# Third x chunk transposed between the slab products, and W4's 64-row rests in pairs of chunks

## The chip, the cores and the metric

The kernel runs on one NeuronCore of a Trainium2 chip. The metric is the device time of one execution in microseconds, the median over the runs shown. TensorE (PE) multiplies, VectorE (DVE) and ScalarE (ACT) work on the results, GpSimd (POOL) does small side work, and SyncE (SP) issues most DMAs.

## The reference

One input x of 2048 rows and 640 columns goes through two branches, and a gate mixes them. Types are bfloat16.

```python
x = A_x                                          # (1, 2048, 640)
g = sigmoid((x * gate_w).sum(-1, keepdims=True))
# branch A: linear attention, 32 heads of 20
q, k, v = split(x @ wqkv)
pq, pk = phi(q), phi(k)                          # phi(t) = (t + 1 if t > 0 else exp(t)) + 1e-6
kv  = einsum("bhsd,bhse->bhde", pk, v); z = pk summed over s
a = (einsum("bhqd,bhde->bhqe", pq, kv) / (einsum("bhqd,bhd->bhq", pq, z) + 1e-6)) @ wo
# branch B: mixer block and MLP
h  = gelu(layernorm(x) @ w1)                     # 640 -> 640
hs = four column groups of h, shifted by +1, -1, +2, -2 rows, @ w2
x1 = x + hs
b  = x1 + gelu(layernorm(x1) @ w3) @ w4          # 640 -> 1728 -> 640
out = g * a + (1 - g) * b
```

## The kernel before, in words

The 2048 rows are 16 chunks of 128. The 640 columns are five slabs of 128 (`DC = 5`). The hidden 1728 columns of the MLP are 13 full slabs (`NF = 13`) and a rest of 64 (`FT = 64`). The order is written out by hand: each engine runs its instructions in the order in which the program records them. Four PSUM buffers (`PP[0]` to `PP[3]`, 1024 float32 columns each) go round in turn by `alloc` and `release`.

**The start.** K = x @ wk needs x with its columns on the partitions (`xT`). The first three chunks are loaded as they are and transposed on PE (`x_tr`, L322 to L328): five transposes into two PSUM buffers, a copy of three of them by DVE (L327) and of two by ACT (L328). All other chunks come by transposing DMAs on SP's queue (`load_xT` in `late_loads`, shown in the profile as L159), between plain loads of x (`load_x`, L156). A one-column memset of `xT` at chunk 3's place (L333) stands ahead of `late_loads`, and the first transposing DMA writes over it, so that DMA waits for DVE to reach the memset. `k_mm(c, p, dc)` (L258, products on L260) multiplies chunk c with slab dc of the K weights `wkg`, in 512 and 130 columns (two of them for the gate and the row sum). The weights' slabs 0 to 2 come on ACT's queue (L166), 3 and 4 on SP's (L173). After the five slabs of a chunk, `k_post` makes phi with ACT (L252) and DVE (L255, L256). A PSUM buffer comes free when DVE is done with it. `g_unit` products (L269, for x-transposed times phi(K)) stand between the chunks.

**The middle.** `kv_unit` (L441) forms the per-head products in six groups of up to 120 columns, the last group having 40; `m_unit` (L455) multiplies each group with its rows of wo. Before the change the sixth group is 120 wide as well: its weights are columns 520 to 639 of wv, and `kvT` of it is padded with zeros to 120 columns. `den_unit` (L468) makes the denominators in tiles of 32 columns of the array, and `rexp_unit` spreads their reciprocals in tiles of 32 rows. `w1_unit` (L420, products on L426) is the first MLP-like product of branch B, `w2_unit` (L557) the second.

**The end.** For each half (t = 0 and 2, eight chunks each) `w3_pair` (L572, products L576) makes twelve slabs of the hidden layer for 512 rows, `w3_rest` (L581, products L585) the thirteenth. `w3_tail` (L590, products L595) makes the rest of 64 columns, for both halves at once, as pairs of 64-column tiles of the array that run side by side. `a_unit(c)` (L602, products L606) is branch A's product for one chunk, scaled by ACT (L609) and added to x1 by DVE (L611). `w4_group` (L620) takes four chunks: 26 products of full height each (`main`, L632: 13 slabs in 512 and 128 columns) and one rest of 64 rows (`rest`, L638), also as pairs of tiles. The rests of all four chunks stand together, at the end of the sums of the first two and the start of those of the last two. `fin` (L615) adds on DVE and sends the output. In the last group the final chunk is split into its 512 and its 128 columns, the second part opened by a product with zero-padded weights `w4z` (L667).

Of the kernel before, what the change touches and what calls it, by code (L numbers as in the profile page):

```python
# [16 lines left out]
def kernel(  # L17
# [14 lines left out]
    P = 128  # L32
# [3 lines left out]
    NCH = S // P  # L36
    DC = D // P
    GW = 120
    NG = 6
    G5 = D - GW  # L40
    gof = [g * GW for g in range(5)] + [G5]
    gw_ = [GW] * 5 + [D - 5 * GW]
    NF = F // P
    FT = F - NF * P
    EPS = 1e-5
# [27 lines left out]
    x_sb = RXH[:, 0:NCH * D].rearrange("p (c d) -> p c d", c=NCH)  # L73
    hsT = RXH[:, NCH * D:NCH * D + DC * (S + 4)].rearrange("p (j s) -> p j s", j=DC)
    h2T = RXH[:, 0:2 * NF * 512].rearrange("p (t f s) -> p t f s", t=2, f=NF)
    KP = 648
    wkg = RA[:, 0:DC * KP].rearrange("p (j d) -> p j d", j=DC)
    o_ = DC * KP
# [20 lines left out]
    o_ += 3 * D  # L99
    gas = [RXH[:, o_ + 2 * i * D:o_ + 2 * (i + 1) * D].bitcast(F32) for i in range(2)]  # L100
    shs = sb("shs", 1024)
    h2x = [RXH[:, 2 * NF * 512:2 * NF * 512 + 512], shs[:, 0:512]]
    w4z = shs[:, 512:640]
    w1x = sb("w1x", DC * P)[:].rearrange("p (j d) -> p j d", j=DC)
    kvT = sb("kvT", 6 * GW)[:].rearrange("p (g d) -> p g d", g=6)
    warm = sb("warm", 512)
# [85 lines left out]
    for f in range(4):  # L192
# [2 lines left out]
                                pattern=[[1, P]], channel_multiplier=-4)  # L195
        nc.gpsimd.affine_select(out=e4, in_=e4, compare_op=ALU.is_ge, fill=0.0, base=3,
                                pattern=[[-1, P]], channel_multiplier=4)
    nc.gpsimd.memset(kvT[0:GW, 5, gw_[5]:GW], 0.0)
    nc.gpsimd.memset(hsT[:, :, 0:4], 0.0)
    nc.gpsimd.memset(hsT[:, :, S:S + 4], 0.0)  # L200

# [83 lines left out]
    def late_loads():  # L285
        load_xT(3, 4)
        load_xT(4, 5)
        load_x(3, 4)
        load_xT(5, 6)
        load_xT(6, 7)  # L290
        load_x(4, 6)
        load_xT(7, 8)
        load_xT(8, 10)
        load_x(6, 9)
        load_xT(10, 11)
        load_xT(11, 13)
        load_x(9, 12)
        load_xT(13, 16)
        load_x(12, 16)
        rows = lambda w, a, b: w[:, a:b].rearrange("(j p) d -> p j d", p=P)  # L300
        sp.dma_start(wq, rows(A_wqkv, 0, D))
        sp.dma_start(w1, rows(B_w1, 0, D))
        sp.dma_start(wv, rows(A_wqkv, 2 * D, 3 * D))
        sp.dma_start(wo6[0:GW, 0:5, :], A_wo[0:5 * GW, :].rearrange("(g r) d -> r g d", r=GW))
        sp.dma_start(wo6[0:GW, 5, :], A_wo[G5:D, :])
        sp.dma_start(w2[:, 0:4, :], B_w2.rearrange("(g c) d -> c g d", c=CG)[0:P])
        for g in range(4):
            sp.dma_start(w2[32 * g:32 * (g + 1), 4, :], B_w2[CG * g + P:CG * (g + 1), :])
        w1g = w1.rearrange("p k (g c) -> p k g c", c=CG)
        w1x4 = w1x.rearrange("p k (g c) -> p k g c", g=4)  # L310
        for g in range(4):
            nc.gpsimd.tensor_copy(w1x4[:, :, g, :], w1g[:, :, g, P:CG])
# [9 lines left out]
    def x_tr(c, a, b):  # L322
        ta, tb = PP[a][:, 0:512].bitcast(BF16), PP[b][:, 0:512].bitcast(BF16)
        for dc in range(DC):
            t, k = (ta, dc) if dc < 3 else (tb, dc - 3)
            nc.tensor.transpose(t[:, k * P:(k + 1) * P], x_sb[:, c, dc * P:(dc + 1) * P], ident[:])  # L326
        nc.vector.tensor_copy(xT[:, 0:3, c * P:(c + 1) * P], ta[:, 0:3 * P].rearrange("p (j s) -> p j s", j=3))  # L327
        act(xT[:, 3:5, c * P:(c + 1) * P], tb[:, 0:2 * P].rearrange("p (j s) -> p j s", j=2), ACT.Copy)  # L328

    for _ in range(3):  # L330
        alloc()
    x_tr(0, 3, 2)
    nc.vector.memset(xT[:, 0, 3 * P:3 * P + 1], 0.0)  # L333
    late_loads()
    x_tr(1, 1, 2)
    k_mm(0, 0, 0)
    k_mm(1, 1, 0)
    k_mm(0, 0, 1)
    k_mm(1, 1, 1)
    x_tr(2, 3, 2)  # L340
    k_mm(2, 2, 0)
    k_mm(2, 2, 1)
    for c in range(3):
# [96 lines left out]

    def kv_unit():  # L441
        p = alloc()
        for g in range(NG):
            w = gw_[g]
            for dc in range(DC):
                mm(PP[p][0:GW, g * P:g * P + w], lhsT=wv[:, dc, gof[g]:gof[g] + GW], rhs=Gp[:, dc, g * GW:g * GW + w],  # L446
                   start=(dc == 0), stop=(dc == DC - 1))
        b0 = PP[p][0:GW, 0:512].rearrange("p (g d) -> p g d", d=P)[:, :, 0:GW]
        nc.vector.tensor_tensor(kvT[0:GW, 0:4, :], b0, bmask[0:GW, :].unsqueeze(1).to_broadcast([GW, 4, GW]),
                                op=ALU.mult)  # L450
        nc.vector.tensor_tensor(kvT[0:GW, 4, :], PP[p][0:GW, 512:512 + GW], bmask[0:GW, :], op=ALU.mult)
        nc.vector.tensor_tensor(kvT[0:GW, 5, 0:w], PP[p][0:GW, 640:640 + w], bmask[0:GW, GW - w:GW], op=ALU.mult)
        release(p)

    def m_unit(g):  # L455
        p = alloc()
        for (n0, n1) in COLS:
            mm(PP[p][0:GW, n0:n1], lhsT=kvT[0:GW, g, :], rhs=wo6[0:GW, g, n0:n1], start=True, stop=True)  # L458
        w = gw_[g]
        act(Mnat[0:w, g, :], PP[p][0:w, 0:D], ACT.Copy)  # L460
        release(p)

    def m_move():
        sp.dma_start(Mscr[0:5 * GW, :].rearrange("(g r) d -> r g d", r=GW), Mnat[0:GW, 0:5, :])
        sp.dma_start(Mscr[5 * GW:D, :], Mnat[0:gw_[5], 5, :])
        sp.dma_start(Mp, Mscr[:, :].rearrange("(q j) d -> q j d", j=DC))

    def den_unit():  # L468
# [60 lines left out]
    w4v = B_w4[0:NF * P, :].rearrange("(f p) d -> p f d", p=P)  # L529
    sp.dma_start(w4[0:FT, NF, :], B_w4[NF * P:F, :])  # L530
    sp.dma_start(w4[FT:2 * FT, NF, :], B_w4[NF * P:F, :])
    nc.gpsimd.memset(w4z[0:FT, :], 0.0)
    sp.dma_start(w4z[FT:2 * FT, :], B_w4[NF * P:F, 512:D])
    sp.dma_start(w4[:, 0:7, :], w4v[:, 0:7, :])
    sp.dma_start(w4[:, 7:NF, :], w4v[:, 7:NF, :])

# [44 lines left out]
    def w3_rest(t):  # L581
# [4 lines left out]
                   rhs=lnxT[:, dc, (t + k) * 512:(t + k + 1) * 512], start=(dc == 0), stop=(dc == DC - 1))  # L586
        act(h2T[:, :, NF - 1, :], PP[p][:].rearrange("p (k s) -> p k s", k=2), ACT.Gelu_apprx_tanh)
        release(p)

    def w3_tail():  # L590
        p = alloc()
        for u in range(2):
            for dc in range(DC):
                for k in range(2):
                    mm(PP[p][FT * k:FT * (k + 1), u * 512:(u + 1) * 512], lhsT=w3[:, dc, NF * P:F],  # L595
                       rhs=lnxT[:, dc, (2 * u + k) * 512:(2 * u + k + 1) * 512], start=(dc == 0), stop=(dc == DC - 1),
                       tile_position=(0, FT * k), skip_group_check=True)
        for u in range(2):
            act(h2x[u], PP[p][:, u * 512:(u + 1) * 512], ACT.Gelu_apprx_tanh)
        release(p)  # L600

    def a_unit(c):  # L602
# [14 lines left out]
                                       op0=ALU.mult, op1=ALU.add)  # L617
        (aq if n0 else sp).dma_start(out2[c * P:(c + 1) * P, n0:n1], oc[:, n0:n1])

    def w4_group(t, g, ahead, last):  # L620
        hx = h2x[t // 2]
        its = [(i, k) for i in (2 * g, 2 * g + 1) for k in range(2)]
        cs = [4 * t + 4 * k + i for (i, k) in its]
        ps = [None] * 4
        oc = [ocs[(ocn[0] + m) % 3] for m in range(4)]
        ocn[0] += 4

        def main(m, parts=COLS):
            i, k = its[m]
            for fc in range(NF):  # L630
                for (n0, n1) in parts:
                    mm(PP[ps[m]][:, n0:n1], lhsT=h2T[:, k, fc, i * P:(i + 1) * P], rhs=w4[:, fc, n0:n1],  # L632
                       start=(m < 2 and fc == 0), stop=(m >= 2 and fc == NF - 1))

        def rest(m, n0, n1):
            i, k = its[m]
            q = slice(FT * k, FT * (k + 1))
            mm(PP[ps[m]][:, n0:n1], lhsT=hx[q, i * P:(i + 1) * P], rhs=w4[q, NF, n0:n1], start=(m >= 2),  # L638
               stop=(m < 2), tile_position=(FT * k, 0))

        ps[0] = alloc()
        main(0)
        a_unit(cs[2])
        a_unit(cs[3])
        ps[1] = alloc()
        main(1)
        ps[2], ps[3] = alloc(), alloc()
        for (ms, (n0, n1)) in zip(((0, 1, 2, 3), (2, 1, 0) if last else (2, 3, 0, 1)), COLS):
            for m in ms:
                rest(m, n0, n1)  # L650
        for m in range(2):
            fin(cs[m], ps[m], 0, D, oc[m])
            release(ps[m])
        main(2)
        fin(cs[2], ps[2], 0, D, oc[2])
        release(ps[2])
        for c in ahead:
            a_unit(c)
        if not last:
            main(3)  # L660
            fin(cs[3], ps[3], 0, D, oc[3])
            release(ps[3])
            return
        main(3, COLS[:1])
        fin(cs[3], ps[3], 0, 512, oc[3])
        ps[3] = alloc()
        mm(PP[ps[3]][:, 512:D], lhsT=hx[:, its[3][0] * P:(its[3][0] + 1) * P], rhs=w4z, start=True, stop=False)  # L667
        main(3, COLS[1:])
        fin(cs[3], ps[3], 512, D, oc[3])

    sq = [(j, 1) for j in range(DC)]
    for t in (0, 2):
        for tt in (t, t + 1):
            for fc in range(0, NF - 1, 2):
                w3_pair(tt, fc)
                pop(ln2_d, 3)
                if sq and not ln2_d:
                    scale_q(*sq.pop(0))
        w3_rest(t)
        if t == 0:  # L680
            assert not ln2_d
            w3_tail()
        while ln2_d:
            pop(ln2_d)
        while sq:
            scale_q(*sq.pop(0))
        a_unit(4 * t)
        a_unit(4 * t + 4)
        w4_group(t, 0, (4 * t + 2, 4 * t + 6), False)
        w4_group(t, 1, (), t == 2)  # L690


# [28 lines left out]
```

## Time and profile before

| what | value |
|---|---|
| time, median of 5 runs | 265.0 us (264.74 to 265.33) |
| the profiled execution's own time | 265.33 us |
| its span, first to last instruction | 263.6 us |
| granted TensorE clock, mean | 1.000 |
| PE busy | 258.8 us, 98% of the span |
| DVE, ACT, POOL busy | 126.8, 109.7, 36.2 us |

The profile is of one execution. The span is what the engines' records cover; the execution's own time is 1.7 us longer. Matmuls overlap in the pipeline and their ends are modelled, so start-to-start times, or the pieces of the chain, tell what a product takes; single durations don't.

### The profile page before, as it was taken

The numbers are of one execution on the slowest core, as the hardware profiler recorded it, in microseconds if no ns is written. First come the engines' busy times: TensorE is split into PE (matmuls) and PEld (weight loads), VectorE is DVE, ScalarE is ACT, GpSimd is POOL, SyncE is SP. The second block draws the span as 40 slices with busy tenths as digits, with TensorE's granted clock in tenths as the row PEclk, the third lists the DMA queues.
The fourth block names the chain that finished last, engine by engine and source line by source line (L and its number), as shares of the span: only waits on it lengthen the run. The fifth ranks groups of instructions, "written<-read, shape, count | busy, mean of one in ns | idle before, by whom it ended". The sixth has DMA issues, their size and how long they took to land.

```text
span 263.6 us, 4185 instructions
## 1 busy us (share of the span) xinstructions
PE 258.8 (98%) x1666; PEld 136.1 (52%) x1666; DVE 126.8 (48%) x227; ACT 109.7 (42%) x163; POOL 36.2 (14%) x120
## 2 busy tenths in 40 slices
PE   7999999999999999999999999999999999999995
PEld 3555555555564445554444455555544445555552
DVE  2387759888995257999920023422310002334133
ACT  3466654555353771334977432102034445202200
POOL 7000043030200000436770000000000000000000
DMA  6799994552242059992552000200200000010011
GB/s 203 156 211 257 367 241 106 100 52 47 52 55 47 4 140 372 339 189 50 100 103 50 0 2 0 75 27 0 77 25 0 0 2 0 0 51 26 25 52 50
DMA packets 42372, 24.07 MB, mean 91 GB/s; under 512 B 31137, under 2 KB 41585, under 8 KB 42353
## 3 DMA queue, kind: packets, MB, share of 16 engines
q1 hardware_dynamic: 41767, 23.28, 36.6%
q10 hardware_dynamic: 586, 0.53, 0.6%
q8 instruction: 13, 0.21, 0.4%
q14 instruction: 6, 0.05, 0.0%
HBM read 12.98 MB, written 3.44 MB: 62 GB/s over the span
## 4 chain that ended last, share of the span: by engine, by line
PE 98%; ACT 0%; DVE 0%; issue 0%
PE pp L632 22%; PE pp L576 20%; PE pp L260 9%; PE pp L606 8%; PE pp L426 8%; PE pp L561 8%; PE pp L269 8%; PE pp L393 8%; PE pp L585 2%; PE pp L316 1%; PE pp L638 1%; PE pp L595 1%; PE pp L446 1%; PE pp L458 1%; PE pp L326 1%; PE pp L472 0%
## 5 line engine op out<-in xcount | busy, mean ns | idle before, releaser
L632 PE MATMUL pp<-RB,RXH 128*128 128x512 bf16 (+1 forms) x416 | 58.6, 299 | 0.0
L576 PE MATMUL pp<-lnxT,RA 128*128 128x512 bf16 x240 | 52.1, 379 | 0.0
L632 PEld LDWEIGHTS <-RXH 128*128 128x128 bf16 x416 | 31.8, 98 | 24.5
L576 PEld LDWEIGHTS <-RA 128*128 128x128 bf16 x240 | 23.4, 98 | 28.1
L578 ACT ACTIVATE RXH<-pp 128x1024 bf16<-128x1024 f32 x24 | 24.3, 1020 | 30.5 <-PE pp L576 30.5
L252 ACT ACTIVATE eb<-pp 128x640 bf16<-128x640 f32 (+1 forms) x26 | 21.4, 829 | 25.0 <-PE pp L393 16.1
L609 ACT ACTIVATE RXH<-pp,g_all 128x640 f32<-128x640 f32 x16 | 12.7, 795 | 45.4 <-PE pp L606 45.4
L611 DVE SCALAR_TENSOR_TENSOR RPK<-RPK,omg,RXH 128x640 f32<-128x640 f32 x8 | 7.1, 884 | 41.4 <-ACT RXH L609 41.4
L269 PE MATMUL pp<-RPK,RXH 128*128 128x512 bf16 (+1 forms) x160 | 25.2, 299 | 0.0
L260 PE MATMUL pp<-RA,RXT 128*128 128x512 bf16 (+1 forms) x160 | 24.2, 303 | 0.5 <-ACT RXT L328 0.5
L393 PE MATMUL pp<-RXT,RA 128*128 128x512 bf16 x100 | 23.2, 379 | 0.0
L606 PE MATMUL pp<-Mp,pqT 128*128 128x512 bf16 (+1 forms) x160 | 23.0, 299 | 0.0
L611 DVE SCALAR_TENSOR_TENSOR RXT<-RXT,omg,RXH 128x640 f32<-128x640 f32 x8 | 7.1, 884 | 32.0 <-ACT RXH L609 32.0
L561 PE MATMUL pp<-w,RXH 128*128 128x512 bf16 (+1 forms) x160 | 21.9, 299 | 0.0
L426 PE MATMUL pp<-lnxT,RB 128*128 128x512 bf16 x80 | 18.3, 379 | 0.0
L269 PEld LDWEIGHTS <-RXH 128*128 128x128 bf16 x160 | 12.7, 98 | 10.4
L260 PEld LDWEIGHTS <-RXT 128*128 128x128 bf16 x160 | 12.6, 99 | 10.2 <-DVE RXT L327 0.8
L606 PEld LDWEIGHTS <-pqT 128*128 128x128 bf16 x160 | 12.3, 98 | 9.8 <-issue 0.4
L561 PEld LDWEIGHTS <-RXH 128*128 128x128 bf16 x160 | 12.3, 98 | 9.6
L393 PEld LDWEIGHTS <-RA 128*128 128x128 bf16 x100 | 11.1, 117 | 9.1
L255 DVE TENSOR_SCALAR eb<-eb 128x640 bf16<-128x640 bf16 (+1 forms) x26 | 9.4, 363 | 11.5 <-ACT eb L252 11.5
L256 DVE SCALAR_TENSOR_TENSOR RPK<-pp,eb 128x640 bf16<-128x640 f32 x16 | 13.2, 824 | 2.1
(112 smaller groups left out, 238.4 us busy)
## 6 DMA issues: line engine op xcount, KB each, us to landing
out_dram<-RXH SPq DMA_DIRECT2D x15, 160.0 KB, 1.8
RA<-in_B_w_dram SPq DMA_DIRECT2D x5, 432.0 KB, 6.8
RA<-in_A_wqkv_dram SPq DMA_DIRECT2D x2, 800.0 KB, 6.8
RB<-in_B_w_dram SPq DMA_DIRECT2D x1, 1120.0 KB, 9.7
RXH<-in_A_x_dram SPq DMA_DIRECT2D x2, 480.0 KB, 4.8
RB<-in_B_w_dram SPq DMA_DIRECT2D x1, 960.0 KB, 11.2
RB<-in_B_w_dram SPq DMA_DIRECT2D x1, 800.0 KB, 8.5
Mp<-Mscr SPq DMA_DIRECT2D x1, 800.0 KB, 4.3
```

Source lines behind the costliest of these rows:

```text
L252: act(e[:, 0:n], src, ACT.Exp)
L256: nc.vector.scalar_tensor_tensor(dst, src, 0.0, e[:, 0:n], op0=ALU.max, op1=ALU.add)
L260: mm(PP[p][:, n0:n1], lhsT=xT[:, dc, c * P:(c + 1) * P], rhs=wkg[:, dc, n0:n1], start=(dc == 0), stop=(dc == DC - 1))
L269: mm(PP[p][:, n0:n1], lhsT=x_sb[:, c, i * P:(i + 1) * P], rhs=pk[:, c, n0:n1], start=(c == 0), stop=(c == NCH - 1))
L393: mm(PP[p][:, tt * 512:(tt + 1) * 512], lhsT=wqp[:, dc, j], rhs=xT[:, dc, t0:t0 + 512], start=(dc == 0), stop=(dc == DC - 1))
L426: mm(PP[p][:, tt * 512:(tt + 1) * 512], lhsT=lh, rhs=lnxT[:, dc, t0:t0 + 512], start=(dc == 0), stop=(dc == DC - 1))
L561: mm(PP[p][:, n0:n1], lhsT=hsT[:, fc, 2 + c * P:2 + (c + 1) * P], rhs=w2[:, fc, n0:n1], start=(fc == 0), stop=(fc == DC - 1))
L576: mm(PP[p][:, k * 512:(k + 1) * 512], lhsT=w3[:, dc, (fc + k) * P:(fc + k + 1) * P], rhs=lnxT[:, dc, t * 512:(t + 1) * 512], start=(dc == ...
L578: act(h2T[:, t % 2, fc:fc + 2, :], PP[p][:].rearrange("p (k s) -> p k s", k=2), ACT.Gelu_apprx_tanh)
L606: mm(PP[p][:, n0:n1], lhsT=pqT[:, j, c * P:(c + 1) * P], rhs=Mp[:, j, n0:n1], start=(j == 0), stop=(j == DC - 1))
L611: nc.vector.scalar_tensor_tensor(x1(c), x1(c), omg[:, c:c + 1], ga, op0=ALU.mult, op1=ALU.add)
L632: mm(PP[ps[m]][:, n0:n1], lhsT=h2T[:, k, fc, i * P:(i + 1) * P], rhs=w4[:, fc, n0:n1], start=(m < 2 and fc == 0), stop=(m >= 2 and fc == N ...
```

## The change

Four places differ.

- At the start, `x_tr(1)` is recorded ahead of the memset and `late_loads`, and `x_tr(2)` goes between the products with slab 0 and those with slab 1 of chunks 0 and 1. On DVE the memset is now behind the copy of the second chunk.
- `kv_unit` and `m_unit` treat the sixth group as 40 wide, without padding.
- `w3_tail` is gone; its products for one half stand at the end of `w3_rest`, once for each half.
- `w4_units` replaces `w4_group`. It takes two chunks: two `a_unit`s, then the four rest products (two chunks, two widths), which open the sums, then the full-height products. The last pair still splits its final chunk into 512 and 128 columns; its second part is opened by a rest product, and `w4z` with its memset and load is gone.

```diff
     x_tr(0, 3, 2)
+    x_tr(1, 1, 2)
     nc.vector.memset(xT[:, 0, 3 * P:3 * P + 1], 0.0)
     late_loads()
-    x_tr(1, 1, 2)
     k_mm(0, 0, 0)
     k_mm(1, 1, 0)
+    x_tr(2, 3, 2)
     k_mm(0, 0, 1)
     k_mm(1, 1, 1)
-    x_tr(2, 3, 2)
     k_mm(2, 2, 0)
     k_mm(2, 2, 1)
...
     def kv_unit():
         p = alloc()
-        for g in range(NG):
-            w = gw_[g]
+        for g in range(6):
+            w = gsz[g]
             for dc in range(DC):
-                mm(PP[p][0:GW, g * P:g * P + w], lhsT=wv[:, dc, gof[g]:gof[g] + GW], rhs=Gp[:, dc, g * GW:g * GW + w],
+                mm(PP[p][0:w, g * P:g * P + w], lhsT=wv[:, dc, g * GW:g * GW + w], rhs=Gp[:, dc, g * GW:g * GW + w],
                    start=(dc == 0), stop=(dc == DC - 1))
...
     def m_unit(g):
         p = alloc()
+        w = gsz[g]
         for (n0, n1) in COLS:
-            mm(PP[p][0:GW, n0:n1], lhsT=kvT[0:GW, g, :], rhs=wo6[0:GW, g, n0:n1], start=True, stop=True)
-        w = gw_[g]
+            mm(PP[p][0:w, n0:n1], lhsT=kvT[0:w, g, 0:w], rhs=wo6[0:w, g, n0:n1], start=True, stop=True)
...
-    nc.gpsimd.memset(w4z[0:FT, :], 0.0)
-    sp.dma_start(w4z[FT:2 * FT, :], B_w4[NF * P:F, 512:D])
...
         act(h2T[:, :, NF - 1, :], PP[p][:].rearrange("p (k s) -> p k s", k=2), ACT.Gelu_apprx_tanh)
         release(p)
-
-    def w3_tail():
...
+        p = alloc()
+        for dc in range(DC):
+            for k in range(2):
+                mm(PP[p][FT * k:FT * (k + 1), 0:512], lhsT=w3[:, dc, NF * P:F],
+                   rhs=lnxT[:, dc, (t + k) * 512:(t + k + 1) * 512], start=(dc == 0), stop=(dc == DC - 1),
+                   tile_position=(0, FT * k), skip_group_check=True)
+        act(h2x, PP[p][:, 0:512], ACT.Gelu_apprx_tanh)
         release(p)
...
-    def w4_group(t, g, ahead, last):
...
+    def w4_units(t, i, last):
+        cs = [4 * t + i, 4 * t + 4 + i]
+        a_unit(cs[0])
+        a_unit(cs[1])
+        ps = [alloc(), alloc()]
+        if last:
+            ps.append(alloc())
+        cc = slice(i * P, (i + 1) * P)
+        for (n0, n1) in COLS:
+            for k in range(2):
+                q = slice(FT * k, FT * (k + 1))
+                p = ps[2] if last and k == 1 and n0 else ps[k]
+                mm(PP[p][:, n0:n1], lhsT=h2x[q, cc], rhs=w4[q, NF, n0:n1], start=True, stop=False,
+                   tile_position=(FT * k, 0))
+        for k in range(2):
+            oc = ocs[ocn[0] % 3]
+            ocn[0] += 1
+            p = ps[k]
+            if last and k == 1:
+                for (p, (n0, n1)) in zip((ps[1], ps[2]), COLS):
+                    for fc in range(NF):
+                        mm(PP[p][:, n0:n1], lhsT=h2T[:, k, fc, cc], rhs=w4[:, fc, n0:n1], start=False,
+                           stop=(fc == NF - 1))
+                    fin(cs[k], p, n0, n1, oc)
+            else:
+                for fc in range(NF):
+                    for (n0, n1) in COLS:
+                        mm(PP[p][:, n0:n1], lhsT=h2T[:, k, fc, cc], rhs=w4[:, fc, n0:n1], start=False,
+                           stop=(fc == NF - 1))
+                fin(cs[k], p, 0, D, oc)
+            release(p)
...
         w3_rest(t)
-        if t == 0:
-            assert not ln2_d
-            w3_tail()
...
-        a_unit(4 * t)
-        a_unit(4 * t + 4)
-        w4_group(t, 0, (4 * t + 2, 4 * t + 6), False)
-        w4_group(t, 1, (), t == 2)
+        for i in range(4):
+            w4_units(t, i, t == 2 and i == 3)
```

More of the change, by code (lines that the diff above doesn't have):

```diff
@@ L38 @@
     GW = 120
[L39 to L42, printed above, removed]
+    gsz = [GW] * 5 + [D - 5 * GW]
     NF = F // P
@@ L75 @@
     h2T = RXH[:, 0:2 * NF * 512].rearrange("p (t f s) -> p t f s", t=2, f=NF)
+    h2x = RXH[:, 2 * NF * 512:2 * NF * 512 + 512]
     KP = 648
@@ L101 @@
     shs = sb("shs", 1024)
-    h2x = [RXH[:, 2 * NF * 512:2 * NF * 512 + 512], shs[:, 0:512]]
-    w4z = shs[:, 512:640]
     w1x = sb("w1x", DC * P)[:].rearrange("p (j d) -> p j d", j=DC)
@@ L197 @@
                                 pattern=[[-1, P]], channel_multiplier=4)
-    nc.gpsimd.memset(kvT[0:GW, 5, gw_[5]:GW], 0.0)
     nc.gpsimd.memset(hsT[:, :, 0:4], 0.0)
@@ L304, in late_loads @@
         sp.dma_start(wo6[0:GW, 0:5, :], A_wo[0:5 * GW, :].rearrange("(g r) d -> r g d", r=GW))
-        sp.dma_start(wo6[0:GW, 5, :], A_wo[G5:D, :])
+        sp.dma_start(wo6[0:gsz[5], 5, :], A_wo[5 * GW:D, :])
         sp.dma_start(w2[:, 0:4, :], B_w2.rearrange("(g c) d -> c g d", c=CG)[0:P])
@@ L451, in kv_unit @@
         nc.vector.tensor_tensor(kvT[0:GW, 4, :], PP[p][0:GW, 512:512 + GW], bmask[0:GW, :], op=ALU.mult)
-        nc.vector.tensor_tensor(kvT[0:GW, 5, 0:w], PP[p][0:GW, 640:640 + w], bmask[0:GW, GW - w:GW], op=ALU.mult)
+        w = gsz[5]
+        nc.vector.tensor_tensor(kvT[0:w, 5, 0:w], PP[p][0:w, 640:640 + w], bmask[0:w, 0:w], op=ALU.mult)
         release(p)
@@ L464, in m_move @@
         sp.dma_start(Mscr[0:5 * GW, :].rearrange("(g r) d -> r g d", r=GW), Mnat[0:GW, 0:5, :])
-        sp.dma_start(Mscr[5 * GW:D, :], Mnat[0:gw_[5], 5, :])
+        sp.dma_start(Mscr[5 * GW:D, :], Mnat[0:gsz[5], 5, :])
         sp.dma_start(Mp, Mscr[:, :].rearrange("(q j) d -> q j d", j=DC))
@@ L588, in w3_rest @@
         release(p)
-    def w3_tail():
         p = alloc()
[L592 to L599, printed above, removed]
+        for dc in range(DC):
[4 more added lines that the diff above has]
+        act(h2x, PP[p][:, 0:512], ACT.Gelu_apprx_tanh)
         release(p)
@@ L618, in fin @@
         (aq if n0 else sp).dma_start(out2[c * P:(c + 1) * P, n0:n1], oc[:, n0:n1])
-    def w4_group(t, g, ahead, last):
[L621 to L669, printed above, removed]
```

## The prediction

> **What bounds the kernel now.** I read the busy shares first, then the chain that ended last, then its pieces around each line that the change touches, and last the start of the span engine by engine.
>
> ```profile
> PE 258.8 (98%) x1666; PEld 136.1 (52%) x1666; DVE 126.8 (48%) x227; ACT 109.7 (42%) x163; POOL 36.2 (14%) x120
> PE 98%; ACT 0%; DVE 0%; issue 0%
> ```
>
> PE is busy for 258.8 of 263.6 us, and the chain is PE nearly everywhere. No other engine's work is worth anything by itself; what counts is how much time PE's own stream takes and where PE waits. So I ask of each edit only whether it makes that stream longer or shorter. The pieces of the chain run from the end of one group to the end of the next, so they show what a group really takes, its overlap taken off:
>
> ```profile
> 78.51 2.16 PE pp L426 x10
> 80.67 1.19 PE pp L472 x20
> 81.86 2.26 PE pp L426 x10
> ...
> 146.79 2.16 PE pp L585 x10
> 148.94 2.28 PE pp L595 x20
> 151.22 2.82 PE pp L606 x20
> 154.05 3.53 PE pp L632 x26
> 157.58 2.72 PE pp L606 x20
> 160.30 3.53 PE pp L632 x26
> 163.83 0.65 PE pp L638 x8
> 164.48 3.64 PE pp L632 x26
> ```
>
> Columns are start, duration, engine, output, line, count. Ten 512-column products take 2.16 us (L426, L585), so one takes 0.216; 26 W4 products (13 of 512 columns, 13 of 128) take 3.53, and 20 of L606 (ten of each width) take 2.72, so a 128-column one takes 0.272 - 0.216 = 0.056. Against these, every stay in a narrower tile shows an excess on both sides. The eight 64-row rests of L638 run in pairs: 2 x 0.216 + 2 x 0.056 = 0.54, and they show 0.65; the 26 products behind them show 3.64 in place of 3.53. That is 0.11 + 0.11 = 0.22 us a stay. The 64-column tail L595 is ten pairs, 2.16, and shows 2.28, and L606 behind it shows 2.82 in place of 2.72: 0.22. The 32-column den (L472) is five rounds of four, 1.08, and shows 1.19, and L426 behind it shows 2.26 in place of 2.16: 0.21. **The price is the same for 5, 10 and 4 rounds, for few and for many rows: it is paid by the stay, not by the work in it.** I take 0.215.
>
> The start is the one place where PE waits:
>
> ```profile
> 5.21 0.37 PE pp L326 x2
> 5.58 1.51 PE pp L260 x8
> 7.09 0.29 PE pp L326 x5
> 7.38 0.02 issue
> 7.41 0.39 ACT RXT L328
> 7.80 0.04 issue
> 7.84 7.25 PE pp L260 x52
> ...
> ```
>
> The third chunk's five transposes (L326, x5) are followed at once by products that need them, so PE stands while they are copied out.
>
> **The change, part by part.**
>
> W4's rests. Before, four stays of eight (the last of seven); after, eight stays of four. The pairs are the same in number. Four more stays: 4 x 0.215 = +0.86. The zero-padded full-height product L667 before the last 13 narrow products goes: the chain gives it 0.06, so -0.06. That the rests now open a group, behind two a_units, adds no wait: their operand h2x is one 512-wide GELU behind the rest's 1.02 us one on ACT, and two a_units (2 x 1.36 us by the 2.72) cover it; an a_unit's own buffer is read by ACT in 0.79 us. Without that cover the first stay of each half would stand up to 0.8 us. The two groups' tail order (512 columns, then 128, then the last two DMAs) is as before.
>
> W3's tail. Once for both halves (20 products) becomes twice ten: the same pairs, one stay more, +0.215.
>
> kv and M of the sixth head group. With 120 columns and zeros these were full tiles; with 40 columns (kv, 128x64 tile) and 40x40 (M, 64x64 tile) they become two new stays, +0.43. The trace has no such small stay, so I bound it. M's two products (512 and 128 columns) keep their time, 0.272, so +0.2 is its price if it switches at all, 0 if it does not. kv's five products come every 55 ns now (30 in 1.67 us, L446), whether 120 or 40 columns stream, so the load of 120 columns sets the pace; with a load of 40 columns the pace lies between 55 and, by the 40 ns steps of the one-column products L379 and L380 in the same chain, something below 40. That takes 0 to 0.15 off kv's stay. I take 55 ns, the row it is nearest to, and +0.43 for both, with ends of -0.15 (no drain, faster loads) and +0.43. The Trainium skill ("TensorE: Matmul & The Clock Gate", LDWEIGHTS) has the load at columns / 1.2 ns: an estimate by it is 33 ns for 40 columns, and the sum would be 0.11 lower; it would also put the present 120 columns at 100 ns, where the trace shows 55, so I keep the row. POOL's memsets and one small SP load that go are off the path: POOL is 14% busy, and w4 lands long before its first use at 154 us.
>
> The start. Before, PE goes on behind k_mm(1,1,0) with two slab-1 pairs (a pair is a k_mm, 512 and 130 columns), the five transposes and the wait, then k_mm(2,2,0). After: transposes, two slab-1 pairs, k_mm(2,2,0). By PE's timeline the last product of k_mm(1,1,0) starts at 6.32, so its slot ends at 6.38; the transposes take 0.29. So they run from 6.38 to 6.66, the slab-1 pairs (0.216 + 0.056 each) to 7.20. DVE's copy of the third chunk (0.36 us, starts 7.30 where the transposes started at 6.93) would end at 6.38 + 0.37 + 0.36 = 7.11, ACT's 0.14 later, 7.25. Before, the products went on 0.91 after the first transpose (7.84 - 6.93); if they need both copies, they go on at 6.38 + 0.91 = 7.29; if DVE's alone, at 7.20. So -0.55 to -0.64; I take -0.57. What is late next: the weights of slabs 0 to 2, issued on ACT's queue from 1.39 to 2.3 us, take 3.2 to 4.9 to land. Slab 1 was used at 6.38 without a stall and is now used at 6.66; slab 2, there by 7.2, was first used at 8.38 and now at about 7.8. The transposes' PSUM buffer is freed by ACT's copy at 6.00, before 6.66. All of ACT's and DVE's chain of phi starts behind PE's products and moves with them.
>
> The moved memset. It stands before the DMA transposes by a write to the same tile, so SP's first of these waits for it. It ran on DVE at 4.88, between the two copies; now it is behind the second (5.10 + 0.36 = 5.46), so it ends near 5.47 in place of 4.93, and SP's queue starts at about 5.5 in place of 4.97. All that is queued behind on SP (nine transposes, six x loads, then the weights) goes 0.53 later, while PE wants it 0.57 sooner: 1.1 us of each margin goes. By the rows:
>
> ```profile
> 4.97 2.61 SPq L159 DMA_TRANSPOSE RXT<-in_A_x_dram  x2
> 7.63 0.58 SPq L156 DMA_DIRECT2D RXH<-in_A_x_dram  x1
> 8.25 2.52 SPq L159 DMA_TRANSPOSE RXT<-in_A_x_dram  x2
> ...
> ```
>
> From issue to landing takes 3.8 (median, 3.3 to 6.0). Chunk 5's transpose, issued at 8.25, lands near 12.1, and PE reaches it 20 products of chunks 3 and 4 after 10.84, at 13.56: a margin of 1.5, now 0.4. Chunk 10's, issued at 14.69, lands at 20.9 and is used at 22.4: also 1.5. Others have 2 or more. So the hold costs nothing, with 0.4 us of cover; if a landing were 0.6 later than that, PE would give back what it gained. It also may gain: the last slabs' loads get the DMA engines alone for half a microsecond, but nobody waits for them.
>
> Sum: +0.86 - 0.06 + 0.215 + 0.43 - 0.57 = +0.87. The profiled execution took 265.33 (span 263.6, 1.7 around it), the highest of the five; against it 266.2. The median is 265.0, and the range of five is 0.6 wide, so the forecast against the median is 265.85.
>
> **Rivals.**
>
> A, not slower: the two small stays of kv and M cost nothing, because a tile of 40 at position 0 needs no drain. For it: the only such narrow product now, L318 at 3.9 us (5 rows), is followed 0.11 us later by a full transpose, no more than the 0.107 between cold transposes. Against: it stands in the cold clock and behind a wait, and all six warm edges of den, tail and rests shown above cost near 0.1. Then 265.0 + 0.44 = 265.44, within the bound. It decides from a price of 0.05 a stay for these two; if the rests' stays cost half besides, it is 265.0. Chance 0.15, and 0.05 more for prices so low that the start's gain wins.
>
> B, the start's gain is lost: the held transposes land too late for chunk 5 or 10, with DMA nine tenths busy in 4 to 16 us. Then PE stands 0.2 to 0.6 at 13 us, and the time is 266.1 to 266.45. Against: landing 0.4 late is more than the spread of the rows at that place (12.1 and 12.8 for two neighbours, each 3.3 to 3.8). Chance 0.14.
>
> C, the clock is released later. The cold steps are 0.107 a transpose and 0.53 a K pair, the warm ones 0.056 and 0.27, and the step falls at about 6.3 us, just before the place to which the transposes move. If they did not count as work, and the release came behind them and the two pairs, it would cost 5 x 0.05 + 2 x 0.26 = 0.8: 266.65. The rows speak against it: the stream before 6.3 is unchanged. Chance 0.03. The Trainium skill ("TensorE: Matmul & The Clock Gate", Part 4) says that transposes don't count as busy for the gate; here those behind 6.3 ran at the warm 56 ns, so they at least keep it.
>
> D, the change doesn't do what it says: the transposes are hidden already or the scheduler moves them back. The order is written out by hand, and PE's list of the changed kernel has them behind k_mm(1,1,0), and the memset behind DVE's second copy; so 0.01.
>
> **How the numbers follow.** The forecast's own case (0.62) is 265.5 to 266.1: +0.87 with kv's pace, the start's ends and 0.2 either way from the five runs. Some 0.2% (0.53 us) is what a measurement of this kernel can tell from no change, so slower begins at 265.53. The forecast's case gives slower 0.54 and same 0.08; B and C give slower 0.17; A gives same 0.14 and faster 0.01; the cheap stays give faster 0.05. D goes to same. In all faster 0.06, same 0.23, slower 0.71. The range reaches down into A, to 265.1, and up through B, to 266.6.
>
> **What would show it.** In the chain after: eight groups of L638's successor with four products each at about 0.38 us in place of 0.65, and 3.64 behind each; two tails of ten at about 1.2; an excess of 0.1 ahead of and behind kv's and M's last products; the 52-product piece that starts at 7.84 now near 7.25, with no ACT piece ahead of it; SP's first transpose near 5.5. I am wrong if PE's stays show less than 0.15 us, if the K products stop between 12 and 15 us by more than the 0.14 they lose there now, or if the start's gain is under 0.4 or over 0.7.

## The result, and the profile after

The changed kernel takes 266.29 us (median of 53 runs, 265.54 to 268.58), the kernel before 265.09 beside it (95 runs). The ratio is 1.0043, 95% interval 1.0034 to 1.0051: slower by 1.1 us, where 265.85 against 265.0, +0.85, was forecast. The range held it (265.1 to 266.6). The profiled execution has a span of 264.7 us in place of 263.6. Lines moved: rests L638 are L622, W4's full products L632 are L637 (L631 in the last chunk), a_unit L606 is L596, the tail L595 is L586, kv L446 is L441, M L458 is L455, the K products L260 are L255, transposes L326 are L321, w1's products L426 are L421, w3_rest's L585 are L579.

The page of the changed kernel, busy time and chain by engine:

```profile
PE 260.3 (98%) x1666; PEld 135.4 (51%) x1666; DVE 127.2 (48%) x227; ACT 109.8 (41%) x163; POOL 35.8 (14%) x118
PE 98%; DVE 1%; ACT 0%; issue 0%
```

The same number of products as before, and 1.5 us more of PE. The chain in order of time shows where (start, duration, engine, output, line, count):

```profile
76.50 1.65 PE pp L441 x30
78.16 2.26 PE pp L421 x10
...
89.29 0.65 PE pp L455 x4
89.94 4.42 PE pp L421 x20
...
146.74 2.16 PE pp L579 x10
148.90 1.20 PE pp L586 x10
150.10 2.82 PE pp L596 x20
152.92 0.38 PE pp L622 x4
153.30 7.17 PE pp L637 x52
160.47 2.72 PE pp L596 x20
163.19 0.38 PE pp L622 x4
163.57 7.17 PE pp L637 x52
```

Each group of four rests takes 0.38 where its two pairs stream for 0.27, and the 52 products behind it 7.17 where 52 took 7.06: 0.11 on each side, eight times. The tail of ten takes 1.20 for five pairs (1.08), and the a_unit behind it 2.82 in place of 2.72, now twice. M's four products go from 0.55 to 0.65 and the 20 behind them from 4.32 to 4.42. Only kv (L441) is not longer in itself, 1.65 in place of 1.67; its 0.10 shows on the products behind, 2.26.

The start of the chain, and SP's queue by its timeline:

```profile
5.58 1.07 PE pp L255 x4
6.65 0.38 PE pp L321 x5
7.03 7.72 PE pp L255 x56
```

```profile
5.51 2.62 SPq L155 DMA_TRANSPOSE RXT<-in_A_x_dram  x2
8.17 0.58 SPq L152 DMA_DIRECT2D RXH<-in_A_x_dram  x1
8.80 2.53 SPq L155 DMA_TRANSPOSE RXT<-in_A_x_dram  x2
```

ACT's copy is gone from between the transposes and the products. The piece of 56 products begins at 7.03 with the four of the slab-1 pairs; by PE's records the third chunk's first product starts at 7.50, where it was 7.84. The gain here is 0.34, not the 0.57 of the sum, and under the 0.4 that the prediction named as a sign of being wrong.

One word on the clock, which the rest needs. Early in the span, transposes start 0.107 us apart and 512-column products 0.43, later 0.056 and 0.216. I call the two paces half and full clock, because they differ by a factor of two. The profile's own row of the granted clock reads 1.00 in both stretches, so that it is the clock is inferred from the paces.

### The profile page after: what moved, and what is told of

Its sections match the earlier page's. It is cut to its first block, busy times and chain, and to the rows that moved or that the text cites. A ratio compares the mean times of both kernels' runs of the same rounds, so it can differ in the third digit from the quotient of the medians.

```text
span 264.7 us, 4180 instructions
## 1 busy us (share of the span) xinstructions
PE 260.3 (98%) x1666; PEld 135.4 (51%) x1666; DVE 127.2 (48%) x227; ACT 109.8 (41%) x163; POOL 35.8 (14%) x118
## 4 chain that ended last, share of the span: by engine, by line
PE 98%; DVE 1%; ACT 0%; issue 0%
PE pp L637 20%; PE pp L570 20%; PE pp L255 9%; PE pp L421 8%; PE pp L596 8%; PE pp L555 8%; PE pp L264 8%; PE pp L388 8%; PE pp L579 2%; PE pp L622 1%; PE pp L631 1%; PE pp L311 1%; PE pp L586 1%; PE pp L455 1%; PE pp L441 1%; PE pp L321 1%
## 5 line engine op out<-in xcount | busy, mean ns | idle before, releaser
L637 PE MATMUL pp<-RB,RXH 128*128 128x512 bf16 (+1 forms) x390 | 54.4, 299 | 0.0
L637 PEld LDWEIGHTS <-RXH 128*128 128x128 bf16 x390 | 29.6, 98 | 24.2 <-issue 2.1
L255 PE MATMUL pp<-RA,RXT 128*128 128x512 bf16 (+1 forms) x160 | 24.4, 304 | 0.0
L596 PE MATMUL pp<-Mp,pqT 128*128 128x512 bf16 (+1 forms) x160 | 23.1, 299 | 0.0
L421 PE MATMUL pp<-lnxT,RB 128*128 128x512 bf16 x80 | 18.3, 380 | 0.0
L264 PEld LDWEIGHTS <-RXH 128*128 128x128 bf16 x160 | 12.7, 98 | 10.4
L255 PEld LDWEIGHTS <-RXT 128*128 128x128 bf16 x160 | 12.6, 99 | 9.5 <-DVE RXT L329 0.3
L596 PEld LDWEIGHTS <-pqT 128*128 128x128 bf16 x160 | 12.2, 98 | 10.0 <-issue 0.8
L555 PEld LDWEIGHTS <-RXH 128*128 128x128 bf16 x160 | 12.3, 98 | 9.6
L606 DVE SCALAR_TENSOR_TENSOR RXH<-pp,omg,RXT 128x640 bf16<-128x640 f32 x8 | 7.1, 884 | 19.8 <-PE pp L637 19.8
L606 DVE SCALAR_TENSOR_TENSOR RXH<-pp,omg,RPK 128x640 bf16<-128x640 f32 (+2 forms) x9 | 7.3, 809 | 19.1 <-PE pp L637 17.2
```

The source lines that it names most:

```text
L255: mm(PP[p][:, n0:n1], lhsT=xT[:, dc, c * P:(c + 1) * P], rhs=wkg[:, dc, n0:n1], start=(dc == 0), stop=(dc == DC - 1))
L264: mm(PP[p][:, n0:n1], lhsT=x_sb[:, c, i * P:(i + 1) * P], rhs=pk[:, c, n0:n1], start=(c == 0), stop=(c == NCH - 1))
L421: mm(PP[p][:, tt * 512:(tt + 1) * 512], lhsT=lh, rhs=lnxT[:, dc, t0:t0 + 512], start=(dc == 0), stop=(dc == DC - 1))
L555: mm(PP[p][:, n0:n1], lhsT=hsT[:, fc, 2 + c * P:2 + (c + 1) * P], rhs=w2[:, fc, n0:n1], start=(fc == 0), stop=(fc == DC - 1))
L596: mm(PP[p][:, n0:n1], lhsT=pqT[:, j, c * P:(c + 1) * P], rhs=Mp[:, j, n0:n1], start=(j == 0), stop=(j == DC - 1))
L606: nc.vector.scalar_tensor_tensor(oc[:, n0:n1], PP[p][:, n0:n1], omg[:, c:c + 1], x1(c)[:, n0:n1], op0=ALU.mult, op1=ALU.add)
```

## A ledger that the start's luck does not touch

The third chunk's first product (the ninth K product) is a mark in every trace. From it on, profiles of kernels with the same W4, tail and head group repeat to 0.01 us, however long their starts took, if PE is in full clock at the mark. So that stretch measures the stays, and the mark's own time measures the start. The one profile in half clock at the mark is that of e8 (253.69); in e10 the ninth K product is another one, a slab-2 product of chunk 0, and its stretch is 252.86. All in us:

| kernel | from the mark to the last PE product | last PE product to the span's end |
|---|---|---|
| before; again (e11); new start alone (e1, e7) | 252.87; 252.86; 252.87, 252.87 | 2.91 |
| W4 in pairs (e2, e5) | 253.66, 253.66 | 3.05, 3.04 |
| sixth group 40 wide (e3) | 253.16 | 2.90 |
| tail twice (e4, e12) | 253.09, 253.09 | 2.91, 2.90 |
| changed kernel; again (e9) | 254.18; 254.18 | 3.04; 3.03 |
| changed kernel, stays cut in two (e6) | 255.88 | 3.06 |

The parts are +0.79, +0.29 and +0.22, in sum +1.30; the whole is +1.31.

## The experiments

**e1: the new start alone**, in the kernel before.

```diff
     x_tr(0, 3, 2)
+    x_tr(1, 1, 2)
     nc.vector.memset(xT[:, 0, 3 * P:3 * P + 1], 0.0)
     late_loads()
-    x_tr(1, 1, 2)
     k_mm(0, 0, 0)
     k_mm(1, 1, 0)
+    x_tr(2, 3, 2)
     k_mm(0, 0, 1)
     k_mm(1, 1, 1)
-    x_tr(2, 3, 2)
```

> The kernel before with the new start alone (the third chunk's transposes between the slab-0 and slab-1 products, the memset behind the second copy). By the prediction's step the K products with the third chunk go on 0.55 to 0.64 us sooner and nothing is given back: 264.4 to 264.5 where before is 265.0. By the changed kernel's trace, where they went on at 7.50 in place of 7.84, the gain is 0.34: 264.7. Rival one, the transposes hold back the release of the clock: the cold spacing (0.107 us a transpose) reaches into this start's transposes again, up to about 6.7 us, as in the changed kernel. Rival two, the release moves from one execution to the next whatever the order: it may fall anywhere near 6.3 to 6.7 here. If the held transposing DMAs land too late, a PE gap of 0.2 us or more shows between 11 and 23 us.

264.81 us; ratio 0.9981, interval 0.9968 to 0.9995: faster by 0.5. Nothing is given back later, 252.87 from the mark on. The mark is at 7.54. PE came to full speed late again: the first four of these transposes start 0.107 apart.

**e2 and e5: W4 in pairs of chunks alone.** w4_units of the changed kernel in the kernel before, with the joint tail:

```diff
-        a_unit(4 * t)
-        a_unit(4 * t + 4)
-        w4_group(t, 0, (4 * t + 2, 4 * t + 6), False)
-        w4_group(t, 1, (), t == 2)
+        for i in range(4):
+            w4_units(t, i, t == 2 and i == 3)
```

In `w4_units`, `h2x[t // 2]` stands in place of `h2x`.

> The kernel before with W4 in pairs of chunks alone: eight stays of four rests, the tail still joint, the sixth head group still padded, the old start. A price by the stay (0.215 us): 4 x 0.215 - 0.06 = +0.80, 265.8 to 265.9 where before is 265.0, and each group of four rests shows 0.38 us with 0.1 more on the products behind it. A price by the work in it (half the rests, half the price): no change, 265.0. If the changed order of sums, outputs and buffers costs anything besides, PE shows gaps at W4 that are not at the edges of the rests.

> The kernel of e2 again, since its interval was wide (1.0031 to 1.0079). By the price by the stay +0.80 in PE's stream and 0.1 in the span's end, 1.003 to 1.0035; if pairs of chunks cost something that PE's stream doesn't show, 1.005 again.

1.0055 (1.0031 to 1.0079), then 1.0034 (1.0008 to 1.0060): 1.5 and 0.9 us. The trace is the same in both: +0.79 of PE and 0.13 to 0.14 in the span's end, 0.93. That is 1.0035, inside both intervals, so the price by the stay holds. The chain of e2:

```profile
152.84 1.36 PE pp L603 x10
154.19 0.38 PE pp L629 x4
...
```

**e3: the sixth head group 40 wide alone** (gof, padding and the memset of kvT gone, `[0:w]` in kv_unit and m_unit, as in the change).

> The kernel before with the sixth head group 40 wide alone, old start and old W4. By the prediction +0.43; by the changed kernel's trace kv costs 0.08 (two edges of about 0.1, less five steps that go from 55 to 29 ns) and M 0.20: +0.28, 265.3 where before is 265.0. By the rival that a tile of 40 at position 0 needs no drain: -0.15 to 0.

1.0023 (1.0006 to 1.0039), and +0.29 in the trace. The small tiles do pay. Its chain:

```profile
76.87 1.65 PE pp L442 x30
...
89.65 0.65 PE pp L455 x4
...
```

M pays 0.20 in full. In kv the two edges are there, 0.09 longer from the last full product to the first narrow one and 0.06 out of the last, with 0.01 more on the product behind. But the four steps between the five narrow products take 0.118 in place of 0.196 (42 ns, then 25 three times; before, 31, then 55 three times), so kv costs 0.08.

**e4 and e12: the tail twice**, `w3_tail` called with one half at a time.

```diff
-        if t == 0:
-            assert not ln2_d
-            w3_tail()
+        w3_tail((t // 2,))
```

> The kernel before with W3's 64-column tail made once for each half, old start, W4 in fours. A price by the stay: +0.21, 265.2 where before is 265.0, each tail of ten showing 1.20 us and the a_unit behind it 2.82. A price by the work: no change, 1.14 and 2.77.

> The kernel of e4, for another profile of the old start, with the same two answers as e11. From the third chunk's first product to the span's end 256.0 again, 0.22 more than in the kernel before.

1.0011 (0.9989 to 1.0034): the times alone can't tell it from no change. The trace can: +0.22 both times, and in the chain of e4 the tail of ten and what is behind it read as forecast.

```profile
149.39 1.20 PE pp L595 x10
150.59 2.82 PE pp L606 x20
```

**e6: each stay cut in two**, in the changed kernel. The 512-column pair opens the sums, the 128-column pair moves between the two chunks' products.

```diff
-        for (n0, n1) in COLS:
-            for k in range(2):
-                ...
+        rests(0, 512, (True, True))
         for k in range(2):
...
+                if k == 0:
+                    rests(512, D, (False, True))   # closes k = 0, opens k = 1
                 fin(cs[k], p, 0, D, oc)
```

> The changed kernel with each of its eight stays of four rests cut in two: the 512-column pair ahead of the sums, the 128-column pair between the two chunks' sums. The same products, eight stays more, of one pair each. A price by the stay: 8 x 0.215 = +1.7 over the changed kernel's 266.2, 267.9, or 1.0107 of before. A price by the work: no change, 266.2. A price that grows with the pairs in a stay: something between.

267.95 us, 1.0089 of before (1.0056 to 1.0121). In the trace +1.70 over the changed kernel for eight stays more, 0.213 each, with the same products. The chain:

```profile
153.50 0.32 PE pp L622 x2
153.82 2.01 PE pp L640 x14
...
157.46 0.16 PE pp L622 x2
157.62 3.64 PE pp L640 x26
```

A pair of 0.216 takes 0.32 and a pair of 0.056 takes 0.16, and the products behind pay another 0.1. A price by the work is out.

**e7: the transposes moved, without the hold.** As e1, with the memset and late_loads left ahead of x_tr(1).

> The kernel before with the third chunk's transposes moved alone: the memset and the transposing DMAs stay ahead of the second chunk's. SP's first of them at 4.97 again. If the hold costs nothing (the prediction's step), as e1, 0.998 of before. If the hold was worth something (the DMA engines free for the weights, DVE's second copy not delayed by the memset's 0.06), slower than e1 by up to 0.1 us. If the hold cost something that e1's gain hid, faster than e1.

264.62 us; 0.9976 (0.9950 to 1.0002). The intervals of e1 and e7 overlap nearly whole; a difference of 0.1 us can't be seen. SP's first transpose is back at 4.98, and from the mark on e1 and e7 take the same time, so the hold's 0.53 us cost nothing there.

**e8: own PSUM banks for each transposed chunk, and slab 2 of chunk 0 ahead of the third chunk's products**, on e1.

```diff
-        ta, tb = PP[a][:, 0:512].bitcast(BF16), PP[b][:, 0:512].bitcast(BF16)
+        ta, tb = PP[a][:, 0:512].bitcast(BF16), PP[b][:, 512:1024].bitcast(BF16)
...
-    x_tr(0, 3, 2)
-    x_tr(1, 1, 2)
+    x_tr(0, 3, 3)
+    x_tr(1, 1, 1)
...
-    x_tr(2, 3, 2)
+    x_tr(2, 3, 3)
     k_mm(0, 0, 1)
     k_mm(1, 1, 1)
+    k_mm(0, 0, 2)
     k_mm(2, 2, 0)
     k_mm(2, 2, 1)
-    for c in range(3):
+    for c in (1, 2):
         k_mm(c, c, 2)
```

> The start of e1 with two more edits: slab 2 of chunk 0 goes ahead of the third chunk's products, which takes the 0.09 us stall that the changed kernel still shows there, and each x_tr writes two banks of one PSUM buffer, so that the second chunk's last two transposes don't wait for ACT's copy of the first (0.41 us at 4.75 to 5.21). Stay price and all else as before. Expected by the rows: the 0.41 us come at the half clock and are worth between half and all, so -0.55 - 0.09 - 0.2 to 0.4: 264.0 to 264.2, 0.9965 of before. If the clock's release falls at a time of its own, the earlier start puts more of the products in front of it, and the gain is nearer to half. If DVE's copies or slab 2's weights (landed at 7.2 us) come too late, the gain of the second edit is lost.

A miss: 265.05 us, 0.9988 (0.9962 to 1.0013). The wait only changed its place. In its waits between 4 and 12 us (engine, line, who was waited for: us, times, longest):

```profile
ACT RXT L328 <- DVE RXT L327: 3.4, 2, 2.3
PEld L326 <- DMA RXH<-in_A_x_dram: 0.9, 1, 0.9
PEld L260 <- DVE RXT L334: 0.4, 1, 0.4
PE pp L260 <- ACT RXT L328: 0.2, 1, 0.2
```

Ten transposes now run without a break, but the copies of one chunk share one buffer, and ACT's starts only when DVE's has ended (5.18 behind 5.14). In the kernel before, with two buffers, ACT's copy starts at 4.78 inside DVE's, 4.57 to 4.93. Products with chunk 1 wait for them until 6.14. PE's clock in this execution stayed at half until 10.4 us.

**e10: slab 2 of chunk 0 ahead of the third chunk's products**, on e7.

> The start of e7 (transposes moved, no hold) and slab 2 of chunk 0 ahead of the third chunk's first product. The 0.09 us stall in front of that product should be gone, and nothing else changes: 264.3 to 264.5 where before is 265.1, 0.9975 of before; with the clock's release and the loads' landing as they fall, anything from 0.995 to 0.999. If slab 2's weights land after about 7.4 us, the stall only moves in front of the product with slab 2.

265.0 us, 0.9981 (0.9956 to 1.0007). No better than e7. In its profile the third chunk's load landed at 7.09, and PE stood for that instead; then it stood 0.18 in front of the product with slab 2, whose weights landed at 8.10. So the trace can't tell what the 0.09 us were worth where the loads come in time. The versions with the new start and the old rest (e1, e7) are the best measured, about 0.5 us under the kernel before.

**e9 and e11: the two kernels again.**

> The changed kernel again. PE's stream from the third chunk's first product to the last product should be 1.31 us longer than in the kernel before (254.2 against 252.9) whatever the clock's release does, and the span's end 0.13 longer. With 0.55 to 0.6 gained at the start that is +0.9, 1.0034 of before; if something that the trace doesn't show is lost besides, 1.0043 again.

> The kernel before, for one more profile of the old start. In e6, e8, e9 and e10, all with the new start, the load of the third x chunk landed at 6.8 to 7.1 us; in the five profiles with the old start it landed at 5.3 to 5.4. If the late landing comes with the execution and not with the order, it may show here too, and PE then waits for slab 1's weights (landed 0.2 after the chunk) in front of the products with slab 1. If it comes with the new order, it stays at 5.3. From the third chunk's first product on nothing changes: 255.78 us to the span's end.

e9: 266.57 us, 1.0029 (1.0007 to 1.0051); the two medians themselves lie further apart, 266.57 against 265.17. The same 254.18 from the mark on. e11 has one run (264.81) and was made for its profile. It is in full clock from 5.3 us on, and so is e7, so these two show the start without the clock in it. The chain of e11, the old start:

```profile
5.49 1.09 PE pp L260 x8
6.58 0.29 PE pp L326 x5
6.87 0.02 issue
6.89 0.39 ACT RXT L328
7.29 0.04 issue
7.33 0.70 PE pp L260 x4
```

and of e7, the new one:

```profile
5.49 0.55 PE pp L260 x4
6.03 0.28 PE pp L326 x5
6.31 1.72 PE pp L260 x12
```

Both come to 5.49 with the same work behind them. The mark is at 7.33 in e11 and at 6.78 in e7: 0.54 us gained.

## Why the prediction was right, and where its sizes were off

**The stays, right.** W4's four more stays and the product that goes: forecast +0.80, measured +0.79 (e2, e5). The tail: forecast +0.215, measured +0.22 (e4, e12). The claim that the price goes by the stay was the step to doubt, and e6 settled it: 0.213 each with half of the work in it. The Trainium skill ("TensorEngine Tiling (Array Packing)", Key Properties) says that a change of tiling mode drains TensorE; it gives no price, and the price here is 0.1 us at each edge (0.06 out of kv's).

**kv and M, mis-sized.** Forecast +0.43, measured +0.29. M pays its 0.20, so rival A (tiles of 40 at position 0 need no drain) is out. The term that failed is kv's, 0.08 in place of 0.215, and under the 0.15 a stay that the prediction named as a sign of being wrong: I kept the 55 ns of 120-column loads, and the four steps came every 29 ns on the mean, 0.08 less; the way out of the tile cost 0.06 where M's costs 0.09. The estimate by the Trainium skill ("TensorE: Matmul & The Clock Gate", LDWEIGHTS), 33 ns, was nearer than my row; its 100 ns for 120 columns stays contradicted by the 55. I had the right bound (0 to 0.15 off) and took the wrong end.

**The start, right in size at full clock, short in the pair of profiles.** Forecast -0.55 to -0.64, and -0.54 in e7 against e11. That is one pair of executions, chosen for its clock. Of the two ways left open, the products went on 0.91 after the first transpose (5.87 to 6.78 in e7), as if they needed both copies. The profiles of before and after showed 0.34 because the clock came to full speed about 0.45 us later in the second: the third chunk's transposes begin at 6.45, not at the 6.38 of the sum, and the first four start 0.107 apart, which together cost 0.2. That looks like rival C, but other profiles speak against the order as its cause: with the old start the slow spacing lasted to about 5.3 us in e11, 6.3 in the first profile and 7.1 in e4. With the new start it came by 5.3 in e7 and at about 6.8 in e1 and in the first profile of the changed kernel. The moment moves with the execution. The runs don't show what sets it.

**The hold, right.** Chunk 5's transpose landed at 12.15, issued at 8.80, less than the 3.8 behind its issue that I had allowed, and was not needed before 13.2; rival B's gap at 13 us is in no trace.

**Left out: the span's end.** All kernels with W4 in pairs take 0.13 us more from the last product to the end (3.04 against 2.91). I had called the last chunk's tail unchanged. DVE's and ACT's last steps are equally long in the traces; the rest is behind the last DMA's issue. By the traces of before and after, 0.05 of it lies between that issue and the last landing (1.53 and 1.58) and 0.08 behind the landing (0.97 and 1.05). The cause stays open.

**Left out: the third x chunk itself.** I checked the weights' landings and not that of the chunk that now comes 0.5 us earlier. Its load is issued at 1.72 us. In the seven profiles with the old start it landed at 5.3 to 5.6; in the seven with the new start at 5.3 to 5.6 three times, and at 6.8 to 7.1 four times (e6, e8, e9, e10). Then PE waits for it, as the chain of e9 shows:

```profile
1.72 5.11 DMA RXH<-in_A_x_dram
6.83 0.05 issue
6.88 0.45 PE pp L321 x5
7.33 1.72 PE pp L255 x12
```

Its mark is at 7.80, 0.47 later than e11's in the same clock: in such an execution the gain is gone against an old start whose load came in time. But in the same four profiles the weights of slab 1 landed 0.2 behind the chunk (7.02 in e9), and the old start uses them at 5.87 in e11, so with such landings it would stand too. An estimate from these rows: it would go on at about 7.05 and need the 1.46 that e11 takes from there to its mark, so 8.5, and the new start would still be 0.7 ahead. No profile shows this.

The load is issued before anything differs in the order of the two programs, so chance is likely, but the profiles don't settle it. The four late ones were taken on two chips, and of the experiments with the old start only e5 was profiled on one of them (in time, as e7 was there). So chip and order are not told apart.

**The sum.** With the measured terms: +0.79 + 0.22 + 0.29 + 0.13 - 0.54 = +0.89, against +0.87 forecast; the short kv (0.14 less) and the long end (0.13 more) nearly cancel, which is luck. Of 265.09 that is 1.0034, inside the interval of e9 and at the lower end of the first one (1.0034 to 1.0051). The lowest times of the two kernels, 264.61 and 265.54, lie 0.93 apart, close to this sum, and the medians 1.20. This suggests that the 0.25 us up to the interval's middle belong to executions other than the fastest, in which the start gains less than 0.54. Whether the clock or the landings do it is open.

## What to carry to other kernels

Count how often PE changes its tile size, not how much work is in the narrow tiles: here a stay cost about 0.21 us whether it held one pair of products or ten, so putting them together (rests of more chunks, both halves' tail) or padding a small group to a full tile is worth as much as the stays it removes, less what the wider tile's products cost (kv's stay came to 0.08, because its narrow products follow faster). A wait at the start is best costed from two profiles in which PE goes at the same pace; pick a mark behind it and keep the time ahead of the mark and the time behind it in separate accounts. When a step is moved forward, check the landing of everything that it reads, its own input first.

## What the runs showed of the hardware that was not expected

- Loads of 40 columns in a 128x64 tile let products of 40 columns follow every 25 ns behind a first step of 42 (e3); loads of 120 columns in a full tile every 55 ns behind a first step of 31 (before).
- A stay in a narrower tile cost 0.213 us with one pair of products in it, 512 or 128 columns wide, as with two (e6 against the changed kernel).
- The moment at which PE's spacing halves differed by nearly 2 us from one execution to the next with the same start (about 5.3 in e11, 7.1 in e4), and was 10.4 us in e8, where PE had stood for 0.23 and 0.30 us between 5.8 and 7.2. Where it had halved before, it stayed so over waits of 1.30 us (e6) and 0.84 us (e9).
- Transposes on PE came every 56 ns in full clock, 107 ns before it.
- One and the same load, issued at 1.72 us, landed after 3.5 to 3.9 us in ten profiles and after 5.1 to 5.4 in four.
